# A fused linear attention and MLP mixer: weight loads on ScalarE's queue, eleven clamps on GpSimd, denominators spread without DRAM

## The chip, the cores and the metric

The kernel runs on one core of a Trainium2 chip. The metric is the device time of one execution in microseconds (us). The engines are TensorE (PE; its weight loads are PEld), VectorE (DVE), ScalarE (ACT), GpSimd (POOL) and SyncE (SP). SPq and ACTq are the queues of SP and ACT, from which DMAs are issued.

## The reference

The first half is a linear attention over 8 batches, 8 heads, 576 positions and 64 dimensions, the second a mixer on its output with two token matrices and two channel matrices.

```
def phi(x):                                   # on q and on k
    proj = x @ w_phi                          # 64 -> 128
    proj = proj - max(|proj|) over the features
    return concat(exp(proj), exp(-proj))      # 256 features
kv = phi(k)^T @ v;  z = sum of phi(k) over the positions
x  = (phi(q) @ kv) / (phi(q) @ z + 1e-6)      # (8, 576, 512)
h  = relu(x^T @ w_tok1) @ w_tok2;  u = x + h^T          # 576 -> 256 -> 576
out = u + relu(u @ w_ch1) @ w_ch2                       # 512 -> 1536 -> 512
```

The four mixer matrices come as 64-bit floats.

## The kernel before

**Streams.** The program is written as five generators that `weave` (line 1037) interleaves: `keys` (673) makes phi(k) and kv, `queries` (790) phi(q) and the quotients, `token_stream` (1004) the token mixer, `load_weights` (569) the mixing weights, `channel_stream` (1011) the channel mixer in 18 blocks of 256 positions with six pairs of 128 hidden channels each. Work on heads goes in pairs, 32 of them. The first 7 pairs (`PLAIN`) multiply in plain fp32; the others split every operand in a high and a low fp32r part and do three matmuls per product (`mm3`, 507).

**Order.** Every instruction is first recorded as an `Op`. `arrange` (273) then simulates the engines with the durations of `cost` (197) and gives each queue, SP's among them, a fixed order; all instructions are issued through line 174, so the profile names them by tiles. For the engines other than PE a ready instruction's turn is its time plus its stream's entry in `HEAD` (249). DMAs share one modelled bus, `bus` (427 to 429). An instruction recorded first on a tile is its opener, and no other instruction on that tile is placed before the opener. Waits between engines are semaphores; each queue runs strictly in its order.

**Weights.** `convert` (543) turns a chunk of 64-bit floats into two fp32r tiles. There are 31 chunks: 7 small ones for the token matrices (tiles raw, bits, w_h, w_l), then 24 of 128x512 for the channel matrices (rawc, bitsc, wc). Per chunk: SP loads it; ACT takes the absolute value of the upper words; POOL clamps them between two constants; DVE shifts and masks, then puts in the sign and the low word in two three-operand steps; ACT makes the high part, POOL the low part by a subtraction. Four rotating buffers hold the raw chunks of the channel matrices, so a load waits until DVE has read the chunk four places earlier. The channel mixer cannot start on a pair of hidden channels until its weights are there, and holds them for the rest of the run.

**Denominators.** `numerators` (849) leaves two tiles u0 and u1 for a pair of heads and a segment of w = 320 or 256 positions. Each holds 64 rows of a head's numerators, and the other 64 rows all hold the denominators of the other head. Lines 872 to 878 load one denominator row of each into the DRAM tile row, load that tile as 128 rows of w/64 values (few), take the reciprocals on DVE, store them to the DRAM tile inv, and load that back broadcast over 64 rows twice; POOL then multiplies u0 by u1 into xt. The PE transposes of the token mixer (px) read xt.

**Start and end.** w_phi is loaded twice, into the lower and upper rows of wp, by ACT's queue, recorded after POOL's memsets of the same tile. `down_proj` (976) adds a pair of hidden channels to two accumulators a0 and a1, each of two 128-row blocks of output channels; `leave` (985) adds each accumulator to the residual in one DVE operation and stores it.

Of the kernel before, what the change touches and what calls it, by code (L numbers as in the profile page):

```python
# [8 lines left out]
F32 = mybir.dt.float32  # L9
F32R = mybir.dt.float32r  # L10
U32 = mybir.dt.uint32
I64 = mybir.dt.int64
AF = mybir.ActivationFunctionType
ALU = mybir.AluOpType
# [3 lines left out]
P = 128  # L18
B, H, S, D = 8, 8, 576, 64
NP = H // 2  # L20
F = 128
# [3 lines left out]
NC_, NE, NT = C // P, E // P, T // P  # L25
# [14 lines left out]
LEAST, MOST = 2.0 ** -15, 122879.9921875  # L40
# [156 lines left out]
def cost(op):  # L197
    outs, ins = op.parts()
    o = outs[0] if outs else None
    n = 1  # L200
    for d in (o or ins[0]).shape[1:]:
        n *= d
    op.shut, op.work = False, 0.0
    if op.name == "dma_start":
        n = 4.0
        for d in (o or ins[0]).shape:
            n *= d
        op.bytes, op.small = n, n < 20000
        return 250.0 if n < 2000 else 335.0 if n < 4000 else 400.0 if n > 5e5 else 560.0
    if op.unit == "tensor":  # L210
        if op.name == "transpose":
            op.work = n / 1.8
            return 110.0
        op.work = n / 2.4 * (1 if op.args[2].root.dtype == F32R else 4) * (op.args[1].hi - op.args[1].lo > D and op.args[0].hi - op.args[0].lo > D or 0.5)
        if op.args[2].root.dtype == F32R:
            return max(114.5, 0.45 * n + 3)
        return 2 * max(111.0, 0.833 * n + 2.5)
    if op.unit == "vector":
        if op.name == "reciprocal":
            return 145 + 6.28 * n  # L220
        if op.name == "tensor_reduce":
            n = 1
            for d in ins[0].shape[1:]:
                n *= d
            return 145 + 1.05 * n
        op.shut = not any(x.root.psum for x in outs + ins)
        return 145 + (0.53 if op.shut and len(ins) == 1 else 1.05) * n
    if op.unit == "scalar":
        if any(x.root.psum for x in ins):
            return 160 + 0.85 * n + (90 if len(ins) > 1 else 0)  # L230
        return 200 + 0.82 * n
    if op.name == "memset":
        return 100 + 0.85 * n
    return 190 + 2.1 * n


# [9 lines left out]
    return FIRST.get(op.unit, (0, 0, -1, 0, -1))[op.stream] * 1e6 + pri  # L246


HEAD = (0,2e3,-1e3,1e4,-5e3)


def urge(op, t):
# [20 lines left out]
def arrange(ops):  # L273
# [77 lines left out]
    ready = {u: [] for u in units}  # L351
    soon = {u: [] for u in units}
    clock = {u: 0.0 for u in units}
    bus, held, loaded = [0.0], {"vector": 0.0, "gpsimd": 0.0}, [-1e9]
    tiles = {}
    slow, beats, spent = [True], [0], {}

# [36 lines left out]
    while count < len(ops):  # L394
# [30 lines left out]
        if op.name == "dma_start":  # L425
            t = max(t, BEGIN)
            clock[u] = t + op.cost
            bus[0] = max(t + op.cost, bus[0]) + op.bytes / RATE
            op.end = bus[0] + LANDING[0 if op.small else 1]
        elif u == "tensor":  # L430
            beat(t)
            pace = 2.0 if slow[0] else 1.0
            c = max(op.cost * pace if op.args[2].root.dtype != F32R or op.name == "transpose" else
                    max(op.cost, (op.cost - 4) * pace), LOAD * pace)
            rows = (op.args[1].lo, op.args[1].hi, op.args[0].lo, op.args[0].hi)
            if op.name == "transpose" or rows[1] - rows[0] == rows[3] - rows[2] == P:
                t = max([t, *(end + TURN for end in tiles.values())])
                tiles.clear()
                clock[u] = t + c
            else:  # L440
                t = max(t + (0 if tiles else TURN), tiles.get(rows, 0.0))
                tiles[rows] = t + c
                clock[u] = t + 14
            op.end = t + c + FILL
            spend(t, t + c, op.work * pace)
        else:
            op.end = t + op.cost
            if op.shut or u == "gpsimd":
                other = held["gpsimd" if u == "vector" else "vector"]
                op.end = max(op.end, other + op.cost - HOLD)  # L450
                held[u] = op.end
            clock[u] = op.end
# [24 lines left out]
def mixer_kernel(ctx, tc, qk, qkp, vals, w_phi, w1, w1t, w2, wc1, wc2d, out):  # L477
# [36 lines left out]

    ident = cst.tile([P, P], F32, name="ident")
    make_identity(real, ident.made())
    ones = cst.tile([P, D], F32, name="ones")
    nc.gpsimd.memset(ones, 1.0)
    eps = odd.tile([P, 2], F32, tag="eps", name="eps", bufs=1)
    for j in range(2):  # L520
        nc.gpsimd.memset(eps[D - j * D:P - j * D, j:j + 1], 1e-6)
        nc.gpsimd.memset(eps[j * D:j * D + D, j:j + 1], 0.0)
    wp2 = st.tile([P, 2, F], F32R, tag="wp2", name="wp2", bufs=1)
    wp = cst.tile([P, 2, F], F32, name="wp")
    for j in (1, 0):
        rows = slice(j * D, j * D + D)
        nc.gpsimd.memset(wp[rows, 1 - j], 0.0)
        nc.scalar.dma_start(wp[rows, j], w_phi)
    for j in range(2):
        rows = slice(j * D, j * D + D)  # L530
        split(wp2[rows, 0], wp2[rows, 1], wp[rows, j], nc.vector, nc.vector)
# [6 lines left out]
    wc1_l = cst.tile([P, NC_, E], F32R, name="wc1_l")  # L538
    wc2 = []

    nstage = [0]

    def convert(hi, lo, src, name, tag=None):

        w, n = hi.shape
        if tag is None:
            tag = f"late{nstage[0] % STAGES}"
            nstage[0] += 1
        raw = wk.tile([P, 4, 256], U32, tag=tag, name=f"raw{name}", bufs=3 if tag == "xt1" else 1)
        raw = raw.rearrange("p a b -> p (a b)")[:w, :2 * n]  # L550
        nc.sync.dma_start(raw.bitcast(I64), src)
        raw = raw.rearrange("p (n two) -> p n two", two=2)
        top, low = raw[:, :, 1], raw[:, :, 0]
        m = wk.tile([P, 512], U32, tag="bits", name=f"bits{name}", bufs=3)[:w, :n]

        nc.scalar.activation(m.bitcast(F32), top.bitcast(F32), AF.Abs)
        nc.gpsimd.tensor_scalar(m.bitcast(F32), m.bitcast(F32), LEAST, MOST, op0=ALU.max, op1=ALU.min)
        nc.vector.tensor_scalar(m, m, 3, 0x3FFFFFF8, op0=ALU.logical_shift_left, op1=ALU.bitwise_and)
        nc.vector.scalar_tensor_tensor(m, top, 0xC0000000, m, op0=ALU.bitwise_and, op1=ALU.bitwise_or)
        nc.vector.scalar_tensor_tensor(m, low, 29, m, op0=ALU.logical_shift_right, op1=ALU.bitwise_or)  # L560
        split(hi, lo, m.bitcast(F32), nc.scalar, nc.gpsimd)
# [287 lines left out]
    def numerators(i, k, j, qps):  # L849
# [15 lines left out]
        if j == 1:  # L865
            if b not in xts:
                xts[b] = [wk.tile([P, NC_, SEG[0][1]], F32, tag="xt0", name=f"xt0_{b}", bufs=3),
                          wk.tile([P, NC_, SEG[1][1]], F32, tag="xt1", name=f"xt1_{b}", bufs=3)]
            x, (u0, u1) = xts[b][k][:, p], (both[0], both[1])
            row, inv = (dr.tile([2, w], F32, tag=t, name=f"{t}{i}_{k}") for t in ("row", "inv"))  # L870
            few = odd.tile([P, 8], F32, tag="few", name=f"few{i}_{k}")[:, :w // D]
            nc.sync.dma_start(row[:1], u0[D:D + 1])
            nc.sync.dma_start(row[1:], u1[:1])
            nc.sync.dma_start(few, row.rearrange("r (p c) -> (r p) c", c=w // D))
            nc.vector.reciprocal(few, few)
            nc.sync.dma_start(inv.rearrange("r (p c) -> (r p) c", c=w // D), few)
            nc.sync.dma_start(u1[:D], inv[:1].to_broadcast([D, w]))
            nc.sync.dma_start(u0[D:], inv[1:].to_broadcast([D, w]))
            nc.gpsimd.tensor_tensor(x, u0, u1, op=ALU.mult)
            if k == sides(i)[1]:  # L880
                attended.add(i)
# [91 lines left out]
        nc.vector.scalar_tensor_tensor(gl, ph, 0.0, gh.bitcast(F32), op0=ALU.max, op1=ALU.subtract)  # L973
        return gh, gl

    def down_proj(acc, ep, gh, gl):
        for a in range(2):
            for k in range(2):
                e = 2 * ep + k
                for c in (2 * a, 2 * a + 1):  # L980
                    cs = slice(c * P, (c + 1) * P)
                    mm3(acc[a][:, c % 2], (wc2[e][:, 0, cs], wc2[e][:, 1, cs]), (gh[:, k], gl[:, k]),
                        e == 0 and c % 2 == 0, e == NE - 1, group_ok=True)

    def leave(acc, segs):
        for k in range(2):
            d = 0
            for b, t, o, n, s in segs:
                v = t[:, 2 * k:2 * k + 2, o:o + n]
                nc.vector.tensor_tensor(v, acc[k][:, :, d:d + n], v, op=ALU.add)  # L990
                nc.sync.dma_start(out[b, :, 2 * k:2 * k + 2, s:s + n], v)
                d += n

    def segments(i):
# [16 lines left out]
    def channel_stream():  # L1011
        accs, segs, prev = {}, {}, None
        n = NE // 2
        for i, ep in [(i, ep) for i in range(B * S // CH) for ep in range(n)] + [(None, None)]:
# [9 lines left out]
            if prev is not None:  # L1024
                j, e, gh, gl = prev
                yield from until(lambda: 2 * e + 1 in loaded)
                if e == 0:
                    accs[j] = [ps_a.tile([P, 2, CH], F32, tag=f"a{k}", name=f"acc{j}_{k}") for k in range(2)]
                down_proj(accs[j], e, gh, gl)
                yield 2.6  # L1030
                if e == n - 1:
                    leave(accs.pop(j), segs.pop(j))
                    yield 0
            if i is not None:
                prev = (i, ep, *g)
# [88 lines left out]
```

## Time and profile before

| | us |
|---|---|
| median of 3 runs (1112.25 to 1116.04) | 1115.82 |
| the profiled execution | 1115.77 |
| its span, first to last instruction | 1113.9 |
| PE busy | 1078.9 |
| DVE, ACT, POOL busy | 672.9, 594.9, 601.0 |

The span is what the trace covers; the profiled execution's own time is 1.9 us more. Busy times are sums over an engine's instructions. Matmuls overlap in the pipeline, so a busy PE need not be at its full rate; the number of matmuls in a stretch, in brackets in the views of stretches, says more.

### The profile page before, as it was taken

To read this page: it belongs to the slowest core of one execution; us is meant where nothing else is said; L and a number is where in the kernel's file an instruction comes from. 1 tells how busy PE (TensorE), PEld (TensorE's weight loads), DVE (VectorE), ACT (ScalarE), POOL (GpSimd) and SP (SyncE) were. 2 spreads that over 40 slices of the span, in tenths; PEclk is the share of its full clock that TensorE was granted. 3 is DMA by queue.
4 is the path that set the end of the run, shared out by engine and by line. 5 is a ranking of instruction groups with operands and counts; after the bars stand their busy time and mean duration, and the time that the engine had idled before them with its cause. 6 is when DMAs were issued, how large, how long until landed. Compare 5 with 4: busy or idle time off the path is not lost.

```text
span 1113.9 us, 23838 instructions
## 1 busy us (share of the span) xinstructions
PE 1078.9 (97%) x8862; PEld 1024.5 (92%) x8862; DVE 672.9 (60%) x1454; ACT 594.9 (53%) x1632; POOL 601.0 (54%) x709
## 2 busy tenths in 40 slices
PE   7999788999999999999999999999999999999998
PEld 6888777798999999999999999999999999999998
DVE  6788766786665657666676676666666653221111
ACT  4767355666656656665656665565665644211110
POOL 3475888566656656566565666656665643001110
PEclk9999998999999999999999999999999999999999
DMA  5556331122211211212121221212121101000000
GB/s 177 151 141 174 118 120 47 51 55 49 51 46 46 55 55 46 62 43 64 46 47 42 55 55 29 66 55 54 43 65 43 40 17 38 1 20 20 20 21 20
DMA packets 60165, 65.41 MB, mean 59 GB/s; under 512 B 27344, under 2 KB 47056, under 8 KB 60048
## 3 DMA queue, kind: packets, MB, share of 16 engines
q1 hardware_dynamic: 59744, 63.48, 21.1%
q8 instruction: 70, 1.15, 0.4%
q14 instruction: 47, 0.39, 0.1%
q10 hardware_dynamic: 304, 0.40, 0.1%
HBM read 54.12 MB, written 9.73 MB: 57 GB/s over the span
## 4 chain that ended last, share of the span: by engine, by line
PE 82%; DMA 7%; POOL 4%; DVE 3%; issue 1%; ACT 1%; SPq 0%; ACTq 0%; POOLq 0%; DVEq 0%
PE h L174 24%; PE acc L174 24%; PE pn L174 7%; PE pkv L174 7%; PE pa L174 4%; PE ph L174 4%; PE ppk L174 4%; PE ppq L174 3%; DMA u<-inv 3%; PE pt L174 3%; DMA inv<-few 2%; POOL bitsc L174 2%; PE px L174 1%; DMA few<-row 1%; DVE bitsc L174 1%
## 5 line engine op out<-in xcount | busy, mean ns | idle before, releaser
L174 PE MATMUL acc<-gh,wc 128*128 128x256 f32 x1728 | 333.2, 281 | 1.7 <-ACT gh L174 1.7
L174 PEld LDWEIGHTS acc<-gh,wc 128*128 128x128 f32 x1728 | 274.1, 189 | 3.2 <-ACT gh L174 2.4
L174 PE MATMUL h<-uh,wc_h 128*128 128x256 f32 x864 | 244.4, 283 | 1.5 <-DVE pmq L174 1.1
L174 PE MATMUL h<-ul,wc_h 128*128 128x256 f32 x864 | 242.5, 281 | 2.1 <-POOL ul L174 2.1
L174 PE MATMUL h<-uh,wc_l 128*128 128x256 f32 x864 | 243.8, 282 | 0.0
L174 PE MATMUL acc<-gl,wc 128*128 128x256 f32 x864 | 243.1, 282 | 0.0
L174 DVE SCALAR_TENSOR_TENSOR gl<-h,gh 128x512 fp32r<-128x512 f32 x108 | 74.3, 688 | 156.0 <-ACT gh L174 155.6
L174 PEld LDWEIGHTS h<-uh,wc_h 128*128 128x128 f32 x864 | 164.3, 190 | 3.2 <-issue 1.5
L174 PEld LDWEIGHTS h<-ul,wc_h 128*128 128x128 f32 x864 | 164.2, 190 | 2.6 <-POOL ul L174 2.5
L174 PEld LDWEIGHTS h<-uh,wc_l 128*128 128x128 f32 x864 | 164.2, 190 | 1.1 <-issue 0.8
L174 PEld LDWEIGHTS acc<-gl,wc 128*128 128x128 f32 x864 | 163.3, 189 | 1.6 <-issue 1.5
L174 ACT ACTIVATE gh<-h 128x512 fp32r<-128x512 f32 x108 | 64.6, 598 | 166.0 <-PE h L174 164.5
L174 ACT ACTIVATE qf<-pt 128x256 f32<-128x256 f32 (+1 forms) x256 | 104.4, 417 | 51.0 <-PE pt L174 47.8
L174 ACT ACTIVATE kp<-pmk 128x256 f32<-128x256 f32 (+1 forms) x320 | 107.7, 391 | 43.4 <-DVE pmk L174 14.0
L174 POOL TENSOR_TENSOR ul<-xt,uh 128x192 fp32r<-128x192 f32 (+3 forms) x120 | 61.1, 541 | 119.4 <-ACT uh L174 118.9
L174 POOL TENSOR_TENSOR ql<-qf,qh 128x320 fp32r<-128x320 f32 (+1 forms) x100 | 84.0, 840 | 65.1 <-ACT qh L174 60.9
L174 POOL TENSOR_TENSOR pmk<-partk,mxk 128x256 f32<-128x256 f32 (+1 forms) x125 | 84.9, 684 | 55.8 <-DVE mxk L174 35.1
L174 POOL TENSOR_TENSOR xt<-u,u 128x256 f32<-128x256 f32 (+1 forms) x64 | 54.2, 847 | 82.3 <-DMA u<-inv 80.6
L174 PE MATMUL pn<-qh,kv 128*128 128x320 f32 (+1 forms) x400 | 97.5, 297 | 0.1
L174 POOL TENSOR_TENSOR stk<-raw,stk 64x512 fp32r<-64x512 f32 (+1 forms) x50 | 71.7, 1447 | 41.7 <-ACT stk L174 39.7
L174 POOL TENSOR_TENSOR stq<-raw,stq 64x512 fp32r<-64x512 f32 (+1 forms) x50 | 74.5, 1491 | 26.2 <-ACT stq L174 19.9
L174 ACT ACTIVATE qh<-pt 128x320 fp32r<-128x320 f32 (+1 forms) x200 | 84.7, 424 | 0.1
(113 smaller groups left out, 2386.9 us busy)
## 6 DMA issues: line engine op xcount, KB each, us to landing
raw<-in_qk SPq DMA_DIRECT2D x24, 576.0 KB
rawc<-in_wc SPq DMA_DIRECT2D x24, 512.0 KB
v<-in_vals SPq DMA_DIRECT2D x31, 325.0 KB
u<-inv SPq DMA_DIRECT2D x64, 80.0 KB
u<-inv SPq DMA_DIRECT2D x64, 64.0 KB
out_x<-xt SPq DMA_DIRECT2D x12, 256.0 KB
out_x<-xt SPq DMA_DIRECT2D x16, 192.0 KB
pair<-in_qkp SPq DMA_DIRECT2D x7, 320.0 KB
```

The costliest lines, as they stand in the source:

```text
L174: return getattr(getattr(nc, self.unit), self.name)(*[real(a) for a in self.args], **{k: real(v) for k, v in self.kw.items()})
```

## The change

ACT's queue instead of SP's issues the 31 weight loads. POOL clamps the first 11 chunks only, DVE the other 20. The denominators go straight from the row of u0 or u1 into 64 rows of few each, without the tile row in DRAM. w_phi's loads are recorded ahead of the memsets of the same tile. For the last block of the channel mixer, `down_proj` finishes the blocks of output channels one after the other, and `leave` takes the second accumulator in two parts. The planner gets a dearer clamp on POOL, other entries in `HEAD`, and a modelled bus for each issuing queue.

```
+    if op.name == "tensor_scalar":
+        return 207 + 3.33 * n
     return 190 + 2.1 * n
...
-HEAD = (0,2e3,-1e3,1e4,-5e3)
+HEAD = (0,1e3,-2e3,1e4,-3e3)
...
-            bus[0] = max(t + op.cost, bus[0]) + op.bytes / RATE
-            op.end = bus[0] + LANDING[0 if op.small else 1]
+            bus[u] = max(t + op.cost, bus[u]) + op.bytes / RATE
+            op.end = bus[u] + LANDING[0 if op.small else 1]
...
+    wp2 = st.tile([P, 2, F], F32R, tag="wp2", name="wp2", bufs=1)
+    wp = cst.tile([P, 2, F], F32, name="wp")
+    for j in (1, 0):
+        nc.scalar.dma_start(wp[j * D:j * D + D, j], w_phi)
+    for j in (1, 0):
+        nc.gpsimd.memset(wp[j * D:j * D + D, 1 - j], 0.0)
...
-        nc.gpsimd.memset(wp[rows, 1 - j], 0.0)
-        nc.scalar.dma_start(wp[rows, j], w_phi)
...
-        nc.sync.dma_start(raw.bitcast(I64), src)
+        nc.scalar.dma_start(raw.bitcast(I64), src)
...
-        nc.gpsimd.tensor_scalar(m.bitcast(F32), m.bitcast(F32), LEAST, MOST, op0=ALU.max, op1=ALU.min)
+        turned_in[0] += 1
+        (nc.gpsimd if turned_in[0] < 12 else nc.vector).tensor_scalar(m.bitcast(F32), m.bitcast(F32), LEAST, MOST, op0=ALU.max, op1=ALU.min)
...
-            nc.sync.dma_start(row[:1], u0[D:D + 1])
-            nc.sync.dma_start(row[1:], u1[:1])
-            nc.sync.dma_start(few, row.rearrange("r (p c) -> (r p) c", c=w // D))
+            for rows, src in ((slice(0, D), u0[D:D + 1]), (slice(D, P), u1[:1])):
+                nc.sync.dma_start(few[rows], src)
...
+    def down_proj(acc, ep, gh, gl, last):
+        steps = [(2 * a + c, k) for a in range(2) for k in range(2) for c in range(2)]
+        for c, k in sorted(steps) if last else steps:
...
+    def leave(acc, segs, last):
+        for c, m in [(0, 2), (2, 1), (3, 1)] if last else [(0, 2), (2, 2)]:
             d = 0
             for b, t, o, n, s in segs:
-                v = t[:, 2 * k:2 * k + 2, o:o + n]
-                nc.vector.tensor_tensor(v, acc[k][:, :, d:d + n], v, op=ALU.add)
-                nc.sync.dma_start(out[b, :, 2 * k:2 * k + 2, s:s + n], v)
+                v = t[:, c:c + m, o:o + n]
+                nc.vector.tensor_tensor(v, acc[c // 2][:, c % 2:c % 2 + m, d:d + n], v, op=ALU.add)
+                nc.sync.dma_start(out[b, :, c:c + m, s:s + n], v)
```

## Rows read from the trace of the kernel before

**Rows 1.** The page: span, then busy time, share and instructions per engine.
```profile
span 1113.9 us, 23838 instructions
...
PE 1078.9 (97%) x8862; PEld 1024.5 (92%) x8862; DVE 672.9 (60%) x1454; ACT 594.9 (53%) x1632; POOL 601.0 (54%) x709
```

**Rows 2.** Stretches: busy us (instructions) per engine, granted clock, DMA share, GB/s.
```profile
105.00:187.00 82.00, 68.38 (x479) 63.01 (x478) 58.59 (x95) 39.08 (x87) 68.52 (x50) 0.94 0.35 106
60.00:187.00 127.00, 111.14 (x797) 102.31 (x797) 96.36 (x181) 71.78 (x172) 97.21 (x72) 0.96 0.41 118
...
187.00:973.00 786.00, 780.63 (x6496) 739.57 (x6495) 510.36 (x1123) 465.89 (x1313) 466.96 (x583) 1.00 0.18 47
...
1110.00:1114.00 4.00, 0.00 (x0) 0.00 (x0) 0.69 (x1) 0.00 (x0) 0.00 (x0) 1.00 0.39 131
```

**Rows 3.** Shorter stretches, the same columns (PE, PEld, DVE, ACT, POOL).
```profile
0.00:5.00 5.00, 0.00 (x0) 0.00 (x0) 0.00 (x0) 1.28 (x1) 1.43 (x13) 1.00 0.60 198
...
83.50:111.00 27.50, 26.30 (x199) 24.05 (x197) 23.13 (x50) 21.69 (x57) 16.12 (x13) 1.00 0.61 174
...
115.00:120.00 5.00, 2.86 (x15) 2.47 (x15) 4.27 (x7) 0.00 (x0) 5.00 (x5) 0.83 0.80 229
...
170.00:175.00 5.00, 5.00 (x33) 5.00 (x33) 4.62 (x7) 1.57 (x5) 4.47 (x3) 0.71 0.10 35
```

**Rows 4.** Chain that ended last, first 200 us: start us, us, what.
```profile
1.18 4.94 DMA wp<-in_w_phi
...
112.25 4.32 POOL bitsc L174 x2
```

**Rows 5.** Waits of PE, whole run: us in total, times, longest us.
```profile
PE ppk L174 <- DMA wp<-in_w_phi: 6.2, 1, 6.2
PE px L174 <- POOL xt L174: 4.9, 5, 2.3
```

**Rows 6.** Waits of PE from 187 us on.
```profile
PE px L174 <- POOL xt L174: 1.5, 3, 1.0
```

**Rows 7.** Tile bitsc, 105 to 187 us: ns min/median/max, first and last start.
```profile
L174 DVE SCALAR_TENSOR_TENSOR bitsc<-rawc,bitsc x33: 662/687/1762, 104.6 to 177.4; 128x512 uint32<-128x512 uint32 x33
...
L174 POOL TENSOR_SCALAR bitsc<-bitsc x15: 1907/1916/2467, 106.4 to 170.4; 128x512 f32<-128x512 f32 x15
L174 DVE TENSOR_SCALAR bitsc<-bitsc x15: 411/826/1511, 108.4 to 172.8; 128x512 uint32<-128x512 uint32 x15
```

**Rows 8.** Groups by shape, whole run: busy us, mean ns, idle before.
```profile
L174 POOL TENSOR_SCALAR bitsc<-bitsc 128x512 f32<-128x512 f32 x24 | 49.2, 2059 | 12.2 <-ACT bitsc L174 12.2
...
L174 DVE TENSOR_SCALAR bitsc<-bitsc 128x512 uint32<-128x512 uint32 x24 | 18.6, 776 | 8.4 <-POOL bitsc L174 8.3
...
L174 DVE TENSOR_TENSOR xt<-acc,xt 128x256 f32<-128x256 f32 x16 | 6.0, 418 | 0.8 <-PE acc L174 0.6
```

**Rows 9.** Stretch 105 to 187 us, DVE's instructions on bitsc alone.
```profile
105.00:187.00 82.00, 40.62 (x48) 0.94 0.35 106
```

**Rows 10.** Tile rawc, whole run: its loads, ns min/median/max.
```profile
L174 SPq DMA_DIRECT2D rawc<-in_wc x24: 328/339/960, 37.0 to 157.4; - x24
```

**Rows 11.** Waits of SP's queue, first 200 us.
```profile
SPq L174 <- DVE bitsc L174: 14.5, 12, 5.9
```

**Rows 12.** Chain that ended last, 936 to 960 us.
```profile
937.46 1.10 DMA row<-u
938.61 1.60 DMA few<-row
```

**Rows 13.** Timeline of the start: start us, us, queue, instruction.
```profile
0.73 0.41 ACTq L174 DMA_DIRECT2D v<-in_vals  x1
...
1.18 1.17 ACTq L174 DMA_DIRECT2D wp<-in_w_phi  x2
```

**Rows 14.** Timeline of the end.
```profile
1110.03 0.69 DVE L174 TENSOR_TENSOR xt<-acc,xt 128x512 f32<-128x512 f32 x1 [0.67 <-PE acc L174]
```

**Rows 15.** Waits of all engines, 105 to 187 us.
```profile
DVE bitsc L174 <- POOL bitsc L174: 8.3, 8, 1.8
```

More of the change, by code (lines that the diff above doesn't have):

```diff
@@ L353, in arrange @@
     clock = {u: 0.0 for u in units}
-    bus, held, loaded = [0.0], {"vector": 0.0, "gpsimd": 0.0}, [-1e9]
+    bus, held, loaded = {u: 0.0 for u in units}, {"vector": 0.0, "gpsimd": 0.0}, [-1e9]
     tiles = {}
@@ L522, in mixer_kernel @@
         nc.gpsimd.memset(eps[j * D:j * D + D, j:j + 1], 0.0)
[L523 to L526, printed above, removed]
-        nc.gpsimd.memset(wp[rows, 1 - j], 0.0)
-        nc.scalar.dma_start(wp[rows, j], w_phi)
     for j in range(2):
@@ L539, in mixer_kernel @@
     wc2 = []
-    nstage = [0]
+    nstage, turned_in = [0], [0]
     def convert(hi, lo, src, name, tag=None):
@@ L869, in numerators @@
             x, (u0, u1) = xts[b][k][:, p], (both[0], both[1])
-            row, inv = (dr.tile([2, w], F32, tag=t, name=f"{t}{i}_{k}") for t in ("row", "inv"))
+            inv = dr.tile([2, w], F32, tag="inv", name=f"inv{i}_{k}")
             few = odd.tile([P, 8], F32, tag="few", name=f"few{i}_{k}")[:, :w // D]
-            nc.sync.dma_start(row[:1], u0[D:D + 1])
-            nc.sync.dma_start(row[1:], u1[:1])
-            nc.sync.dma_start(few, row.rearrange("r (p c) -> (r p) c", c=w // D))
+            for rows, src in ((slice(0, D), u0[D:D + 1]), (slice(D, P), u1[:1])):
+                nc.sync.dma_start(few[rows], src)
             nc.vector.reciprocal(few, few)
@@ L974, in up_proj @@
         return gh, gl
[L976 to L986, printed above, removed]
+    def down_proj(acc, ep, gh, gl, last):
+        steps = [(2 * a + c, k) for a in range(2) for k in range(2) for c in range(2)]
+        for c, k in sorted(steps) if last else steps:
+            e, cs = 2 * ep + k, slice(c * P, (c + 1) * P)
+            mm3(acc[c // 2][:, c % 2], (wc2[e][:, 0, cs], wc2[e][:, 1, cs]), (gh[:, k], gl[:, k]),
+                e == 0 and c % 2 == 0, e == NE - 1, group_ok=True)
+    def leave(acc, segs, last):
+        for c, m in [(0, 2), (2, 1), (3, 1)] if last else [(0, 2), (2, 2)]:
             d = 0
             for b, t, o, n, s in segs:
-                v = t[:, 2 * k:2 * k + 2, o:o + n]
-                nc.vector.tensor_tensor(v, acc[k][:, :, d:d + n], v, op=ALU.add)
-                nc.sync.dma_start(out[b, :, 2 * k:2 * k + 2, s:s + n], v)
+                v = t[:, c:c + m, o:o + n]
+                nc.vector.tensor_tensor(v, acc[c // 2][:, c % 2:c % 2 + m, d:d + n], v, op=ALU.add)
+                nc.sync.dma_start(out[b, :, c:c + m, s:s + n], v)
                 d += n
@@ L1028, in channel_stream @@
                     accs[j] = [ps_a.tile([P, 2, CH], F32, tag=f"a{k}", name=f"acc{j}_{k}") for k in range(2)]
-                down_proj(accs[j], e, gh, gl)
+                down_proj(accs[j], e, gh, gl, i is None)
                 yield 2.6
                 if e == n - 1:
-                    leave(accs.pop(j), segs.pop(j))
+                    leave(accs.pop(j), segs.pop(j), i is None)
                     yield 0
```

## The prediction

> **What bounds the kernel now.** I read the page's busy times first: the matmul engine PE is busy 1078.9 of 1113.9 us [rows 1], so no other engine's total can set the time; only PE's own work and the stretches in which it starves can. Next I cut the span into stages [rows 2]. From 187 to 973 us PE is busy 780.63 of 786 us and starts 6496 matmuls, 8.26 a microsecond: no room. After it the channel mixer runs alone, and PE does not idle. From 105 to 187 us there is room: 479 matmuls in 82 us, which at 8.26 a microsecond would be 58.0 us, so 24.0 us are lost there (an estimate: the mix of matmuls differs a little). GpSimd (POOL) is the busiest helper in that stretch, 68.52 of 82 us, against 58.59 for VectorE (DVE) and 39.08 for ScalarE (ACT). Part of the 24 us is clock: the granted clock falls to a mean of 0.83 in 115 to 120 us and 0.71 in 170 to 175 us, so PE ran part of those at its lower level (1.2 instead of 2.4 GHz), after it had stood idle [rows 3].
>
> Third, the chain of waits says who starves PE there: its longest pieces between 109 and 170 us are POOL's work on the weights, for instance 4.32 us for two clamps in a row [rows 4]. PE's own list of waits then gives the rest: 6.2 us at the start for the load of w_phi, and 4.9 us in five waits for the divided attention tile xt [rows 5], of which 1.5 us in three waits come after 187 us [rows 6].
>
> **The clamp.** There are 31 weight chunks, 7 small and 24 of 128x512. The edit leaves 11 clamps on POOL and moves 20 to DVE. Between 105 and 187 us stand 15 POOL clamps, all of them later than the eleventh chunk, 33 DVE three-operand steps and 15 DVE shift-and-mask steps [rows 7]. A POOL clamp takes 2059 ns on average [rows 8], so 15 of them are 30.9 us, and POOL falls from 68.5 to 37.6 us, 0.55 of before. No DVE clamp is in the trace; the nearest row is DVE's shift-and-mask on the same tile, also one input and two constants: 411 ns at best [rows 7], 776 ns on average [rows 8]. The gap of 365 ns is there while POOL works on SBUF beside it. All DVE work on these chunks takes 40.62 us in the stretch [rows 9]; at its best durations it would be 33 x 0.662 + 15 x 0.411 = 28.0 us, so 12.6 us are such excess.
>
> Lower bound: excess stays, each clamp costs 0.776. DVE has 58.6 + 11.6 = 70.2 us. The highest DVE share of a stage in this trace is 23.13 of 27.5 us, 84% [rows 3]; at that the stretch takes 70.2 / 0.84 = 83.6 us, a loss of 1.6 us. Upper bound: the excess vanishes and the clamp costs 0.411: 58.6 - 12.6 + 6.2 = 52.2 us, at 84% 62.1 us, a gain of 19.9 us; PE's own floor of 58.0 us allows 24.0 us. Value taken: the excess follows POOL's load, 0.55 x 12.6 = 6.9 us left, and the clamp costs 0.411 + 0.55 x 0.365 = 0.61 us, 9.2 us in all. DVE: 58.6 - 5.7 + 9.2 = 62.1 us, at 84% 73.9 us: a gain of 8.1 us. The 5 moved clamps before 105 us, where POOL is not the busiest, I take as nothing. What comes late next is DVE itself: behind each clamp stand the exponent maxima and subtractions of the keys and queries.
>
> The Trainium skill bears on this (SBUF — State Buffer, Who interferes with whom): VectorE in a two-port mode, which a one-input constant operation can enter, and GpSimd exclude each other for a whole instruction, and so does a VectorE operation with two SBUF inputs against a GpSimd one that reads. The spread from 411 to 1511 ns [rows 7] agrees. It speaks against the change, since a clamp on VectorE can be locked out too; if every clamp were, the time would be the lower bound's.
>
> **The loads on ScalarE's queue.** 31 loads leave SP's queue for ACT's. An issue of rawc takes 339 ns, 960 at most [rows 10]; 31 x 0.339 = 10.5 us of ACT's time. ACT is idle 127 - 71.78 = 55 us between 60 and 187 us [rows 2], so I take nothing for it; without that cover it is up to 10.5 us. The wait matters more: each load waits until DVE has read the chunk that held the buffer. SP waited 14.5 us for that in 12 waits, the longest 5.9 us [rows 11]. On ACT the queue behind such a wait holds the exponentials, the evictions `u`, the Relu `gh` and the next chunk's abs, and PE waits for these. Bounds: nothing, to 14.5 us lost. I take nothing, since the waits shrink if chunks run faster, and SP's denominators are freed from them.
>
> **The denominators.** Before, two rows go to DRAM and one load spreads them: 1.10 us, then 1.60 us after an issue [rows 12], 2.8 us in all from 937.46 to 940.26. After, two loads of 64 rows each go straight from the SBUF row: one hop of 1.6 us, plus about 0.3 us for the second issue, so about 0.9 us earlier for each of the 64 (pair, segment) steps. SP issues two such DMAs where it issued three. Nearly everywhere PE has other work meanwhile. Bounds: nothing, to the 4.9 us that PE waits for xt. The two waits before 187 us lie in the stretch above; of the other 1.5 us I take 1.0.
>
> Against this edit stands the Trainium skill's advice not to split a transfer into two partition halves, which use the same engines one after the other (DMA: Bandwidth & Descriptors, Rules for kernel authors). No row here shows the split spread; if the halves simply followed each other at 1.6 us, the hop would take 3.2 us and gain nothing, and the sum would lose its 1.0.
>
> **The start.** On ACT's queue the load of v stands ahead of w_phi's two [rows 13], and w_phi lands 4.94 us after 1.18 [rows 4]. The new recording order puts w_phi first. It gains at least v's issue, 0.41 us. At most it lands like a small DMA, and then the first tile of keys decides: 256 KB at the 198 GB/s of the first 5 us [rows 3] are 1.3 us, after the issue at 0.73 and with the 1.10 us that a small transfer takes [rows 12]; PE would start at 3.2 us instead of 6.25, 3.1 us earlier. I take 1.5, about midway, as the tiles behind the first still come when they did.
>
> **The tail.** The last eviction shrinks from 128x512 to 128x256, 0.69 to 0.42 us [rows 14, 8], and its store from 256 to 128 KB; at the 131 GB/s of the last 4 us [rows 2] that is 1.0 us, at twice that rate 0.5. Bounds 0.3 to 1.3; I take 0.7.
>
> **The planner's numbers.** Clamp costs, streams' head starts and one bus per queue reorder every queue. Nothing shows the new order. From 187 us on PE idles only some 5 us, so a better order can win no more; a worse one can lose as much. I take zero, and 5 us on either side.
>
> **Sum:** 8.1 + 1.0 + 1.5 + 0.7 = 11.3 us off the profiled execution's 1115.77 us, which agrees with the median of 1115.82: **1104.5 us**. About 0.5% (5.6 us, so 1110.2 and 1121.4) is what a measurement can tell from no change.
>
> **Rivals.** (a) PE fills the stretch: DVE's excess vanishes with POOL's load. For it: 12.6 us of excess; against: 17 split operations stay on POOL. 1115.8 - 19.9 - 3.2 = 1092.7 us. (b) DVE takes POOL's place: lower bound of the clamp, 1115.8 + 1.6 - 3.2 = 1114.2 us. For it: DVE is already at 72% there and gains work; against: DVE's eight waits for POOL's clamp, 8.3 us [rows 15], go. (c) Slower: ACT stalls in front of its loads. The 14.5 us of SP's waits fall on ACT, and PE idles with it, with the clamp's gain gone as in (b): 1114.2 + 14.5 = 1128.7 us. For it: gh and the exponentials feed PE directly; against: ACT is idle 43% there. It decides from the point where ACT's waits before loads cost PE over 7 us more than the clamp's move frees. (d) The denominators and the start do nothing because other work fills them: 1115.8 - 8.1 - 0.7 = 1107.0 us.
>
> **Chances.** Forecast with (d), 1098 to 1110: 0.46. (a): 0.22. (b): 0.20. (c): 0.12. Forecast and (a) are faster, 0.68; (b) lies within 0.5%, 0.20; (c) is slower, 0.12. The range runs from 1091, beyond which (a) would need all of PE's floor, to 1119, halfway into (c).
>
> **What would show it.** Right: PE's first matmul before 5 us; in the chain of waits POOL's clamps gone between 105 and 187 us; the last weight split ended some 8 us earlier than 187; twenty DVE clamps near 0.6 us; `few` following `u` by one hop; a last eviction of 128x256. Wrong: ACT idle before weight loads with PE idle beside it, DVE over 84% busy in the weight stage with POOL under half, or a later end of the weights.

## The result: 1131 us, slower by 1.5%, and the profile after

The changed kernel takes 1130.95 us (median of 4 runs, 1125.86 to 1134.64) against 1114.03 us for the kernel before on the same chip: ratio 1.0148, interval 1.0126 to 1.0170. The profiled execution took 1125.86 us, the fastest of the four: its span is 10.1 us longer than that of the profile before, so the trace shows some 10 us of a loss of 16.9 us between the medians. In the runs below the kernel before was measured each time beside the edited one, with medians from 1113.1 to 1114.0 us. (Ratios leave disturbed executions out, medians do not; the two can differ by up to 1.6 thousandths.)

The page of the changed kernel, span and busy times, to be set against [rows 1]:

```profile
span 1124.0 us, 23749 instructions
...
PE 1083.3 (96%) x8862; PEld 1029.2 (92%) x8862; DVE 685.3 (61%) x1475; ACT 592.5 (53%) x1632; POOL 562.3 (50%) x689
```

The clamps did leave POOL (601.0 to 562.3 us busy). To see where the time went I count matmuls by stretch: who has started fewer by a given moment is late by the difference at 8.26 a microsecond, the pace of [rows 2]. The first stretch of the kernel before (columns as in [rows 2]):

```profile
0.00:105.00 105.00, 92.95 (x686) 85.25 (x687) 79.36 (x197) 69.23 (x187) 52.97 (x53) 1.00 0.57 158
```

The same stretch and the two after it in the changed kernel:

```profile
0.00:105.00 105.00, 89.24 (x606) 81.25 (x606) 70.14 (x180) 60.94 (x165) 41.25 (x47) 0.95 0.54 148
105.00:187.00 82.00, 71.09 (x515) 66.70 (x513) 65.56 (x124) 44.26 (x101) 33.03 (x31) 0.94 0.36 111
187.00:973.00 786.00, 775.71 (x6445) 734.17 (x6446) 523.57 (x1129) 465.46 (x1316) 475.42 (x589) 1.00 0.18 48
```

Before 105 us 80 matmuls are lost (9.7 us), in part by the clock: the granted clock is 0.95 on average where it was 1.00. Some of the stretch runs at its lower level, 1.2 instead of 2.4 GHz, after PE has stood idle: PE is busy 0.71 of the 2.5 us from 45.0 us, and the next two such pieces have 0.69 and 0.63. Between 105 and 187 us, where [rows 2] had 479, 36 are won back, which the clamp by itself also does in a run below. From 187 to 973 us 51 more are lost (6496 in [rows 2]). Together that is 95 matmuls, 11.5 us.

The chain of waits of the first 190 us was led by POOL's clamps (`bitsc`, 9.5% of it; pieces in [rows 4]). Now 21% of it are the denominators' transfers (`inv<-few` 9.0%, `u<-inv` 8.4%, `few<-u` 3.9%); some pieces:

```profile
39.59 4.34 DMA inv<-few
...
87.72 4.01 DMA u<-inv
...
122.25 5.41 DMA u<-inv
```

And the start, ScalarE's (ACT's) timeline, against [rows 13]: `wp` is first, but four weight loads stand ahead of the load of ACT's function table, and the third and the fourth of them wait:

```profile
0.73 1.19 ACTq L174 DMA_DIRECT2D wp<-in_w_phi  x2
1.96 0.60 ACTq L174 DMA_DIRECT2D v<-in_vals  x1
2.60 1.47 ACTq L174 DMA_DIRECT2D raw<-in_w  x2
6.77 0.48 ACTq L174 DMA_DIRECT2D raw<-in_w1t  x1
8.36 0.34 ACTq L174 DMA_DIRECT2D raw<-in_w  x1
8.72 1.28 ACT L174 ACT_TABLE_LOAD   x1 [8.72 <-DMA v<-in_vals]
10.02 0.72 ACT L174 ACTIVATE kp<-pmk 128x256 f32<-128x256 f32 x2
```

### The profile page after: what moved, and what is told of

Read it like the earlier page. It is cut to its first block, busy times and chain, and to the rows that moved or that the text cites. A ratio compares the mean times of both kernels' runs of the same rounds, so it can differ in the third digit from the quotient of the medians.

```text
span 1124.0 us, 23749 instructions
## 1 busy us (share of the span) xinstructions
PE 1083.3 (96%) x8862; PEld 1029.2 (92%) x8862; DVE 685.3 (61%) x1475; ACT 592.5 (53%) x1632; POOL 562.3 (50%) x689
## 4 chain that ended last, share of the span: by engine, by line
PE 82%; DMA 8%; DVE 4%; POOL 2%; issue 2%; ACT 1%; SPq 0%; ACTq 0%; DVEq 0%; POOLq 0%
PE acc L174 24%; PE h L174 24%; PE pn L174 8%; PE pkv L174 7%; PE ph L174 4%; PE pa L174 4%; PE ppk L174 3%; PE ppq L174 3%; DMA u<-inv 3%; PE pt L174 3%; DMA inv<-few 2%; DMA few<-u 1%; PE px L174 1%; DVE bitsc L174 1%; PE pkt L174 1%
## 5 line engine op out<-in xcount | busy, mean ns | idle before, releaser
L174 DVE TENSOR_TENSOR ks<-ks,kp 128x512 f32<-128x512 f32 (+1 forms) x100 | 81.6, 816 | 7.2 <-ACT kp L174 5.9
L174 DVE TENSOR_TENSOR ql<-qf,qh 128x320 fp32r<-128x320 f32 (+1 forms) x100 | 68.8, 688 | 26.6 <-ACT qh L174 26.3
```

The source lines that it names most:

```text
L174: return getattr(getattr(nc, self.unit), self.name)(*[real(a) for a in self.args], **{k: real(v) for k, v in self.kw.items()})
```

## The experiments

The kernel's order is written by a planner (`arrange`) from its own figures, so every edit changes two things: the work and the order. Two kinds of experiment keep them apart. "Planned anew" means that the edit is made and the planner runs. "Order kept" means that the planner sees the old program, and an operation is then emitted at its old place on another engine, or with other operands. Theories: **order** (the new order costs), **queue** (loads on ACT cost), **clamp** and **hop** (the edits themselves); the expectations add **bus** and **head** (the planner's buses and `HEAD`) and **landing** (its durations of small transfers). The code shows the lines that matter; "..." marks what is left out.

### One part of the change undone, planned anew

Loads on SP again:
```diff
-        nc.scalar.dma_start(raw.bitcast(I64), src)
+        nc.sync.dma_start(raw.bitcast(I64), src)
```


> The changed kernel with the weight loads issued by SP; as nearly all DMAs are SP's then, the planner's bus is in effect one again. Theory BUS: as with one bus, 1105 to 1117 us. Theory QUEUE: 1105 to 1117 us too, and then the kernel with one bus but ACT's queue stays near 1131. Theories HEAD and HOP: 1126 to 1135 us.

Measured: 1118.72 us, ratio 1.0052 (1.0027 to 1.0077): 12.2 us less than the changed kernel, just above the 1117 us of the bus and queue theories, and still slower than before.

The planner's two buses one again:
```diff
-            bus[u] = max(t + op.cost, bus[u]) + op.bytes / RATE
+            bus["sync"] = max(t + op.cost, bus["sync"]) + op.bytes / RATE
```


> The changed kernel, but the planner has one modelled bus for all DMAs again. Theory BUS (the planner, with a bus of its own for SP, counts the small denominator DMAs as landing about 1 us after issue, while in the changed kernel's first 187 us they take a median of 2.4 to 3.4 us; so POOL's, ACT's and SP's queues are ordered for data that comes late): 1105 to 1117 us. Theory QUEUE (ACT issuing the loads, and the loads sharing the DMA engines with the small transfers, costs the time itself): about 1131. Theory HEAD (the new head starts of the streams): about 1131. Theory HOP (the direct denominator loads are slower than the way through DRAM): about 1131.

Measured: 1125.95 us, 1.0096 (1.0079 to 1.0113). Only an order differs, and 5.0 us go, which is neither of the two times expected.

The old figures of `HEAD`:
```diff
-HEAD = (0,1e3,-2e3,1e4,-3e3)
+HEAD = (0,2e3,-1e3,1e4,-5e3)
```


> The changed kernel with the old entries of HEAD. Theory HEAD: 1105 to 1117 us. Theories BUS, QUEUE and HOP: 1126 to 1135 us, as the changed kernel, give or take some 5 us that any new order brings.

Measured: 1133.93 us, 1.0167 (1.0147 to 1.0187). The new entries are not the loss.

The denominators through DRAM again (the old lines of the diff, with the tile `row`):
```diff
...
-            for rows, src in ((slice(0, D), u0[D:D + 1]), (slice(D, P), u1[:1])):
-                nc.sync.dma_start(few[rows], src)
+            nc.sync.dma_start(row[:1], u0[D:D + 1])
+            nc.sync.dma_start(row[1:], u1[:1])
+            nc.sync.dma_start(few, row.rearrange("r (p c) -> (r p) c", c=w // D))
```


> The changed kernel with the denominators through DRAM as before (two rows stored, one load of 128 rows). Theory HOP: 1105 to 1117 us. Theories BUS and QUEUE: 1131 us or more, since there is one more late hop in each chain. Theory HEAD: about 1131 us.

Measured: 1138.46 us, 1.0211 (1.0185 to 1.0238): slower by 7.5 us without the edit, so the hop theory is out.

### One part done alone

The queue, order of before kept (`real` names the engine that an operation is emitted on; its line stands behind the load):
```diff
-        return getattr(getattr(nc, self.unit), self.name)(
+        return getattr(getattr(nc, getattr(self, "real", self.unit)), self.name)(
...
+        nc.ops[-1].real = "scalar"
```


> The kernel before in its own order, every instruction in the place that its planner gave it, but the 31 weight loads are issued by ACT instead of SP. Nothing else is moved. Theory QUEUE-DIRECT (an in-order ACT queue waits at its loads, for a buffer or for an earlier DMA's landing, and the exponentials and evictions behind them wait too): 1120 to 1128 us. Theory ORDER (the queue itself costs nothing; the new places of the other instructions cost it): 1110 to 1117 us.

Measured: 1120.21 us, 1.0047 (1.0030 to 1.0064): 5.2 us by the ratio, 7.0 by the medians, with no order changed.

The clamp, order of before kept (with the line of `real` as above):
```diff
+        turned_in[0] += 1
+        nc.ops[-1].real = "gpsimd" if turned_in[0] < 12 else "vector"
```


> The kernel before in its own order, but the clamps from the twelfth chunk on are done by DVE at the place that they had. The prediction's clamp step: POOL's 20 clamps of 2.06 us go, DVE gains 20 of about 0.6, a gain of some 8 us in 105 to 187 us: 1104 to 1110 us. Rival (DVE takes POOL's place, or the weights are not what holds PE): 1112 to 1118 us.

Measured: 1113.44 us, 0.9999 (0.9980 to 1.0019). Its stretches:

```profile
0.00:105.00 105.00, 95.12 (x695) 87.16 (x696) 80.08 (x205) 70.46 (x190) 43.68 (x48) 1.00 0.58 160
105.00:187.00 82.00, 71.63 (x532) 65.20 (x531) 63.20 (x117) 42.87 (x95) 45.08 (x42) 0.98 0.36 110
187.00:973.00 786.00, 777.05 (x6456) 737.00 (x6456) 506.20 (x1113) 463.25 (x1309) 461.59 (x581) 1.00 0.18 47
```

At 187 us it is 62 matmuls ahead of before, 7.5 us of the 8.1 that the sum gave the clamp; DVE has 63.2 us there (62.1 in the sum). Behind 187 us it gives 40 matmuls (4.8 us) back, and the forecast of this run, 1104 to 1110 us, is missed.

The changed kernel's own order kept, loads emitted on SP (with the line of `real`):
```diff
+        nc.ops[-1].real = "sync"
```


> The changed kernel in its own order, but the weight loads are issued by SP, each at the place in the order that it had. Theory QUEUE-DIRECT: 1116 to 1122 us, near the 1118.7 us of the kernel that was also planned with SP's loads. Theory ORDER: 1128 us or more, as the changed kernel, since the order is the changed kernel's.

Measured: 1129.73 us, 1.0151 (1.0111 to 1.0191). Against 1118.72 us of the same work on the same queues, planned for them: an order alone is worth 11.0 us. In the changed kernel's order leaving ACT's queue saves 1.2 us by the medians, with intervals that overlap: nothing that can be told.

The direct denominator loads alone, planned anew (in the kernel before):
```diff
...
-            nc.sync.dma_start(row[:1], u0[D:D + 1])
-            nc.sync.dma_start(row[1:], u1[:1])
-            nc.sync.dma_start(few, row.rearrange("r (p c) -> (r p) c", c=w // D))
+            for rows, src in ((slice(0, D), u0[D:D + 1]), (slice(D, P), u1[:1])):
+                nc.sync.dma_start(few[rows], src)
```

> The kernel before with the direct denominator loads alone (planned anew). Since undoing them in the changed kernel cost 7.5 us, they should gain here too: 1106 to 1112 us if a hop less is worth something in any order; 1112 to 1117 us if the hop is hidden where the chains are not late already.

Measured: 1132.47 us, 1.0161 (1.0139 to 1.0184). One hop less and 18 us more, where a gain or nothing was expected. The edit changes work and order at once; the run with the order kept, below, tells them apart.

### Is any new order that bad?

A figure of the planner moved by 1 ns:
```diff
-    return 190 + 2.1 * n
+    return 191 + 2.1 * n
```


> The kernel before with one figure of its planner moved by 1 ns: a GpSimd operation is reckoned at 191 + 2.1 n ns instead of 190 + 2.1 n. Every instruction, queue and size is as before; only the order that the planner writes out differs. ORDER theory (any new order costs several us, because the order of before is a lucky one among many nearly equal ones): 1118 to 1132 us. Rival (the planner gives orders of nearly equal time, and it was the wrong times that the change gave it, or the work itself, that cost): 1111 to 1116 us.

Measured: 1117.10 us, 1.0036 (1.0022 to 1.0050).

The kernel before with the new `HEAD`:
```diff
-HEAD = (0,2e3,-1e3,1e4,-5e3)
+HEAD = (0,1e3,-2e3,1e4,-3e3)
```


> The kernel before with only the five figures of HEAD (urgency of the streams on the engines other than TensorE) as in the change. No work changes. ORDER theory: 1118 to 1132 us, as for the 1 ns. Rival, the new figures are better for any kernel: 1105 to 1112 us. Rival, they are the part of the change that costs: over 1125 us here, while the kernel with the 1 ns stays at 1111 to 1116 us.

Measured: 1116.39 us, 1.0025 (1.0007 to 1.0043). Both miss what the order theory expected: in these two, a new order of unchanged work costs 2 to 4 us, not 11 to 18. My theory that the order of before was merely lucky fell; something makes the new orders bad.

The direct loads, order of before kept (the two copies become the loads, at their places, and the load from DRAM goes; `instead` holds an operation's new operands, or none if it is left out):
```diff
             nc.sync.dma_start(row[:1], u0[D:D + 1])
+            nc.ops[-1].instead = (few[:D], u0[D:D + 1])
             nc.sync.dma_start(row[1:], u1[:1])
+            nc.ops[-1].instead = (few[D:], u1[:1])
             nc.sync.dma_start(few, row.rearrange("r (p c) -> (r p) c", c=w // D))
+            nc.ops[-1].instead = ()
```


> The kernel before with its own order kept: the two copies of the denominators to DRAM become the two loads straight into the tile of 128 rows, at their own places in SP's queue, and the load from DRAM is dropped. ORDER theory: the direct loads themselves cost nothing, the time is 1110 to 1114 us (the sum's gain of 1.0 us, or less if SP's issues of 0.47 us in place of 0.24 and 0.34 us eat it). Rival, the direct loads are what made the kernel with them alone, and a new order, 18 us slower: 1122 us or more.

Measured: 1110.58 us, 0.9970 (0.9955 to 0.9985): the same work as the run of 1132.47 us, 21.9 us faster. The two later stretches in the old order,

```profile
105.00:187.00 82.00, 70.89 (x509) 64.19 (x508) 61.54 (x100) 42.38 (x93) 72.26 (x54) 0.96 0.34 104
187.00:973.00 786.00, 779.70 (x6505) 740.03 (x6504) 509.80 (x1117) 464.42 (x1311) 465.77 (x587) 1.00 0.18 47
```

and in the order planned anew:

```profile
105.00:187.00 82.00, 66.29 (x444) 59.84 (x444) 58.45 (x93) 39.06 (x87) 61.56 (x44) 0.92 0.34 102
187.00:973.00 786.00, 771.80 (x6398) 728.15 (x6397) 521.29 (x1125) 466.99 (x1315) 473.05 (x587) 1.00 0.19 48
```

So the planned order loses 65 matmuls in the first and 107 in the second, 20.8 us together. What DVE's reciprocal waited for in the old order, over the whole run (us in total, times, longest us):

```profile
DVE few L176 <- DMA few<-u: 6.7, 10, 1.4
```

And in the order planned anew:

```profile
DVE few L174 <- DMA few<-u: 31.1, 29, 2.9
```

The planner sets the reciprocal where it believes the loads to have landed, and DVE, which works in order, stands there 29 times; in the old order the place was reckoned for two hops, and the one hop is in time. Such waits have no fixed price: DVE waited 41.1 us in 38 there in the kernel before, too, 41.6 us in the changed kernel and 44.1 us with its loads on SP, and these three take 1114 to 1131 us. PE's waits behind 187 us sum to 13.5 us in the order planned anew, 6.1 here and 5.0 before; the first two differ by only 7.4 of the 21.9 us. So through which waits the new order costs its time is not shown. What the planner believes can be read in the code: 250 ns to issue a transfer this small, and 1.0 us from the end of the issue until it lands. The trace of the changed kernel shows for an issue of these loads (ns min/median/max):

```profile
L174 SPq DMA_DIRECT2D few<-u x128: 463/475/887, 23.9 to 940.5; - x128
```

and for the transfers into and out of `few` (KB each, median us from the start of the issue to landing):

```profile
few<-u SPq DMA_DIRECT2D x64, 1.2 KB, 1.8
few<-u SPq DMA_DIRECT2D x64, 1.0 KB, 2.2
...
inv<-few SPq DMA_DIRECT2D x32, 2.5 KB, 1.9
inv<-few SPq DMA_DIRECT2D x32, 2.0 KB, 2.2
```

From the start of an issue of `few<-u` the planner reckons 1.25 us, and the trace shows 1.8 and 2.2.

All of the change but the queue, order of before kept (the clamp and the hop as above, the new last group, and `wp`'s loads first, which are the lines shown):
```diff
...
     order = arrange(nc.ops)
+    first = [op for op in order if op.stream == "" and op.parts()[0] and op.parts()[0][0].root.kw["name"] == "wp"]
+    order = first + [op for op in order if op not in first]
```


> The kernel before with its own order kept, and of the change all but the queue: clamps from the 12th chunk on VectorE, direct denominator loads, the two loads of wp first, the new last group and last evictions. ORDER theory: not slower than before: 1104 to 1113 us (1104 if the gains of the early stretches last to the end as the sum had them, 1110 to 1113 if they are given back behind 700 us as with the clamp alone). Rival, some edit itself costs: 1118 us or more.

Measured: **1104.92 us**, 0.9924 (0.9897 to 0.9952), the fastest of all, 0.8% under the kernel before. Its stretches:

```profile
0.00:105.00 105.00, 97.05 (x720) 89.40 (x721) 84.82 (x209) 73.45 (x196) 45.83 (x50) 1.00 0.57 168
105.00:187.00 82.00, 72.63 (x528) 65.81 (x528) 61.26 (x115) 42.14 (x94) 44.78 (x42) 0.96 0.33 101
187.00:973.00 786.00, 779.15 (x6509) 740.75 (x6508) 507.00 (x1116) 461.82 (x1305) 461.67 (x582) 1.00 0.18 47
```

### The planner's figures put right

```diff
-        return 250.0 if n < 2000 else 335.0 if n < 4000 else ...
+        return 475.0 if n < 2000 else 335.0 if n < 4000 else ...
...
-LANDING, RATE, BEGIN = (1000.0, 1400.0), 210.0, 750.0
+LANDING, RATE, BEGIN = (1800.0, 1400.0), 210.0, 750.0
```

From the start of an issue of `few<-u` that makes 2.28 us, a little over the longer of the two medians, since the profile's landing holds the issue and the planner's does not. The landing figure goes for every transfer under 20 kB, so for `inv<-few` too.

The direct loads alone, planned anew with these:

> The kernel before with the direct denominator loads alone, ordered anew by the planner (as the run that took 1132.5 us), but the planner now reckons what the traces show for them: 475 ns to issue a direct load in place of 250, and 1.8 us until a small transfer has landed in place of 1.0. The work is the same. LANDING theory (the planner's wrong durations of the direct loads make the bad order: VectorE's reciprocal placed before its data can be there): 1110 to 1117 us. Rival (an order planned anew without the hop is bad for another reason, or the orders scatter at random by more than 3 us): 1122 us or more.

Measured: 1113.81 us, 1.0002 (0.9988 to 1.0016), 18.7 us less than with the old figures. The stretch from 105 to 187 us starts 490 matmuls again and the one behind it 6485, PE's waits behind 187 us sum to 7.0 us, and DVE's wait is halved:

```profile
DVE few L174 <- DMA few<-u: 16.8, 21, 2.3
```

The whole change with them:

> The changed kernel, with the same two figures of the planner put right (475 ns, 1.8 us), nothing else. LANDING theory: 1110 to 1118 us, since what is left is the price of ScalarE's queue, 5 us. Rival (the queue of ScalarE and its stalls set the time of the changed kernel): 1124 us or more.

Measured: 1121.94 us, 1.0069 (1.0044 to 1.0095): 9.0 us less than with the old figures, between the two expectations.

The whole change with them, loads on SP:

> The changed kernel with its loads of the mixing weights issued by SP again and the same two figures of the planner put right. LANDING theory: 1104 to 1112 us, near the 1104.9 us that the same edits take in the order of before. Rival: 1116 us or more, as without the two figures (1118.7 us).

Measured: 1108.66 us, 0.9950 (0.9934 to 0.9967): 10.1 us less than the same with the old figures, and faster than before. With the figures put right ACT's queue costs 13.3 us (1121.94 against 1108.66). The kernel before was not planned with these figures, so what they do to an order without the direct loads stays open.

### What the queue costs

All edits and ACT's queue, order of before kept (the run of 1104.92 us with one more line):
```diff
+        nc.ops[-1].real = "scalar"
```

> All edits of the change in the order of before (the run of 1104.9 us) and the loads of the mixing weights issued by ScalarE as well: the whole change without its new order. QUEUE theory (ScalarE's issues and their waits cost 5 to 7 us whatever else is done, as they did alone): 1110 to 1112 us. Rival, the queue costs nothing here because the other edits leave room: 1103 to 1106 us. Rival, it costs more, since the 24 late loads then wait beside the faster stretch: 1114 us or more.

Measured: 1113.55 us, 0.9996 (0.9983 to 1.0008): 8.6 us more than with SP, between two of the expectations. This is the whole change in the order of before: it gains nothing and loses nothing, and the changed kernel's own order takes 17.4 us more. ACT's first exponential goes from 7.08 us without its queue,

```profile
2.59 1.28 ACT L176 ACT_TABLE_LOAD   x1 [2.59 <-issue]
7.08 1.51 ACT L176 ACTIVATE kp<-pmk 128x256 f32<-128x256 f32 x4 [3.21 <-DVE pmk L176]
```

to 10.64 us with it:

```profile
9.34 1.28 ACT L176 ACT_TABLE_LOAD   x1 [9.34 <-DMA v<-in_vals]
10.64 1.33 ACT L176 ACTIVATE kp<-pmk 128x256 f32<-128x256 f32 x4
```

So I tried whether the start is all of it: the first seven loads on SP, the 24 of the channel weights on ACT.
```diff
+        loads[0] += 1
+        nc.ops[-1].real = "sync" if loads[0] < 8 else "scalar"
```


> As the run of all edits in the order of before with ScalarE's queue (1113.6 us), but the first seven loads (w1, w1t, w2) stay on SP, so that ScalarE issues only the loads of the channel weights, from the eighth on, and its table load and first exponential are not held behind the first four. START theory (the queue costs because ScalarE's first exponential goes from 7.08 to 10.64 us): 1105 to 1109 us. Rival (the late loads, issued behind ScalarE's own work and holding it for their completion slots, cost as much): 1110 to 1114 us.

Measured: 1110.46 us, 0.9974 (0.9961 to 0.9987). The start is worth 3.1 us of the 8.6, the 24 late loads 5.5; each takes ACT 0.33 us to issue, 8 us in all. With the queue as the only edit (1120.21 us), ACT's first exponential comes at 9.43 us where it came at 9.39, so there the start can have cost little. POOL's wait before it multiplies into `xt` is the same (34.9 us before 187 us with and without); ACT's delay shows in SP, which waits 21.0 us for ACT's `u` between 60 and 187 us where it waited 11.0.

The same in the changed kernel with the right figures, planned anew:
```diff
+        loads[0] += 1
+        (nc.sync if loads[0] < 8 else nc.scalar).dma_start(raw.bitcast(I64), src)
```


> The changed kernel with the two figures of the planner put right (1121.9 us), the first seven loads on SP again, the others still on ScalarE. START theory: 1108 to 1113 us, within the 3 us that an order scatters of the same kernel with all loads on SP (1108.7 us). Rival, the late loads cost: 1116 us or more.

Measured: 1127.25 us, 1.0113 (1.0094 to 1.0133), 5.3 us more than with all loads on ACT. The start theory fails here: with the late loads on ACT none of the six orders that this planner made comes under 1121 us.

## Why the prediction was wrong

The edits themselves came near the sum: all but the queue, in the old order, gain 9.0 us where 11.3 were forecast, which gives 1104.92 us (forecast 1104.5, from a median of before that was 1.8 higher). That it comes so near is in part luck: the hop brought more than its term, and the clamp alone keeps nothing at the end. The two terms that I had set at nothing did not hold. From the runs' medians: 1104.92; + 13.8 for planning them anew (1118.72), of which 10.1 go with the two figures (1108.66) and 3.7 are about what an order of unchanged work scatters by (2.4 and 3.1 us in the two tried); + 12.2 for the loads on ACT, planned for that: 1130.95.

- **"The planner's numbers … I take zero, and 5 us on either side"** is the step that failed. The reason given, that PE idles only 5 us behind 187 us, bounds what an order can win; it does not bound what one can lose. An order made from durations that are too short, by 0.5 to 0.9 us from the start of an issue to landing (0.2 of it the issue), lost 9 to 19 us in three pairs of runs that differ in these two figures alone. I had costed the shorter hop and not asked who else believes in its duration. That the loss comes about by reciprocals placed before their data, with DVE holding what is queued behind them, is likely but not shown, and which of the two figures matters more was not tried.
- **The loads on ACT's queue** ("I take nothing", bounds 0 to 14.5 us) cost 5.2 to 7.0 us alone and 8.6 beside the other edits in a fixed order, 12.2 in the changed kernel. ACT's idle time, 43% of the stretch from 60 to 187 us, did not cover them. Rival (c), 1128.7 us, came nearest in time, by luck: the clamp's gain, which it gave up, is there, and its mechanism is only a part. At the start ACT waits not for DVE to free a buffer but for earlier transfers. In the trace of the changed kernel its 486 transfers signal eight semaphores in turn, 60 or 61 times each, over both queues, and a load waits until the one eight places earlier in the program has landed: the third weight load is issued at 6.77 us, when the second of `wp` is there, and the fourth at 8.36 us, when `v` is. On SP that holds transfers; on ACT it holds the table load. And in the changed kernel most of the 12.2 us is again order: emitted on SP in the same order it saves 1.2 us, and one bus in the planner saves 5.0. Why the planner does not find a good order with these loads on ACT stays open; it reckons 0.40 us for an issue (0.33 measured), but nothing of the shared semaphores.
- **The clamp** was right to 187 us and not at the end: 7.5 us against 8.1. Alone, in the old order, the 15 DVE clamps from 105 to 187 us take 0.62 us on average (0.58 in the changed kernel), where 0.61 stood (busy us, mean ns, idle before):

```profile
L174 DVE TENSOR_SCALAR bitsc<-bitsc 128x512 f32<-128x512 f32 x15 | 9.3, 622 | 3.4 <-ACT bitsc L174 3.3
```

  POOL's last step on the weights starts at 178.2 us there, 7.7 us earlier than before (185.9), as forecast. In the changed kernel it starts at 193.2 us: the later end of the weights that I had named as a sign of being wrong. Alone the clamp keeps nothing measurable at the end (0.9999); with the other edits in the old order the stretch from 187 to 973 us starts 6509 matmuls and nothing is given back. What gives it back alone I have not shown. To 187 us rivals (a) and (b) are out: alone the clamp starts 53 matmuls more in the stretch than before, and 532 of the 677 that 82 us at 8.26 would hold. DVE's share of the stretch is 77% there and 80% in the changed kernel, but 87% with its loads on SP, above the 84% that I took as the most.
- **The denominators** are worth 3.4 us, not 1.0. The first mistake was to look only at PE's waits for `xt`; DVE's 41.1 us in 38 waits for `few<-row` in the kernel before fell to 6.7 us in 10, though that the gain comes from there is not shown. The Trainium skill's advice against two partition halves (DMA: Bandwidth & Descriptors, Rules for kernel authors) would have taken the gain away. No run here tests it: the issues of the two halves of a step lie 6.8 us apart in the median in the changed kernel and 5.7 us in the old order, so one has mostly landed before the other is issued. A half lands 1.8 us (segments of 320) or 2.2 us (of 256) after its own issue starts in the changed kernel, 1.8 or 2.0 in the old order; my 1.9 us from the first issue on took the halves as issued one behind the other.
- **The start:** PE's first matmul came before 5 us as forecast (3.80 in the changed kernel), but there ACT's first exponential slid from 9.39 to 10.02 us behind the loads. In the old order with the loads on SP the first 20 us start 110 matmuls against 95 before, 1.8 us where 1.5 stood; planned anew with the loads on SP they start 85. The last eviction is 128x256 as forecast; start and tail were not timed by themselves, and of the 9.0 us the 5.6 beside the hop are theirs and the clamp's together.

A queue of its own gave the loads no speed: the median landing of the 24 loads of 512 KB is 4.6 us on SP and 4.4 us on ACT (two runs that differ in nothing but the queue of these). The Trainium skill says as much (DMA: Bandwidth & Descriptors, Issuing engines are not separate DMA queues): transfers from either engine run on the same 16 DMA engines, and only the issue time is saved. Here SP's issue time was saved and ACT's was spent, and PE waits for ACT.

## What to carry to other kernels

Where a planner writes the order, an edit to a transfer is two edits: measure the new transfer and give the planner its figures, or the order is made for a kernel that does not exist. To learn which of the two cost, keep the old order and emit the new work in it; those two runs (1104.92 and 1118.72 us) differ by nothing else. Put transfers on a compute engine's queue only where nothing urgent stands behind them in it, and ask what each of them must wait for.

## What the runs showed of the hardware

A load of 64 partitions from one SBUF row costs its queue 475 ns in the median where the copy of that row to DRAM cost 242, and both halves together 0.95 us of SP, where the three transfers of before (two at 242, one at 343 ns) took 0.83. A clamp of 128x512 costs DVE 0.42 us in the median and 0.59 us on average in the changed kernel, and the four that POOL keeps there take 1.9 to 2.4 us. The table load, which waits for no tile, came at 8.72 us there, behind the transfers that ACT had to issue first; with those on SP, in the old order, it came at 2.59 us.
